# Moving one fetch in the opening, and the queues and buffers of the last regroupings and stores, in a fused Fourier-mixing and SoLU kernel

## The chip, the cores and the metric

The kernel runs on one core of a Trainium2 chip, in float32 throughout. The metric is the time of one execution on the device, in microseconds (us). The kernel before took 1618.07 us, the median of three runs (1616.99, 1618.07 and 1626.45).

## The reference

What is computed, cut to what matters: a circular convolution along the sequence by way of the real Fourier transform, and on its result a two-layer block with a SoLU activation and a layer norm.

```python
X = np.fft.rfft(x, axis=1)                  # x: 8 x 3136 x 256
y = np.fft.irfft(X * F, n=3136, axis=1)     # F = filt_r + 1j * filt_i
h = y.reshape(25088, 256) @ w_in            # d_ff = 1024
sm = exp(h - max(h)) / (sum(exp(h - max(h))) + 1e-9)
solu = h * sm
ln = (solu - mean(solu)) / sqrt(var(solu) + 1e-6) * g_ln
out = ln @ w_out                            # 25088 x 256
```

## The kernel before, in words

**Fourier part.** The sequence of 3136 is split as 49 x 64. Each batch element goes through four stages with two trips to DRAM: a first product with a 49-point table (`first`, matmul L230 or L273, results `d1` in DRAM), then for seven "units" of frequencies `forward` (product with a table `de`, matmul L305, tiles `pb`), `multiply` (by the filter, L326 to L328, tiles `pr`, `pi`, `pt`), `inverse` (L305 again, tiles `pc`, copied out by ScalarE at L343) and `store` (L347, `d2` in DRAM), and last `back` into the rows `y` that the second block reads.

**Opening.** For batch element 0 this runs on its own, ahead of everything else, in an order that is written out by hand (manual schedule). Its first unit's rows `t2` are asked for at L563 (16 DMAs, shared by SyncE's and ScalarE's queues). The other six units' rows are asked for on SyncE's queue at L295 (`y<-d`, 512 KB each, the last 128 KB), in the loop at L565. Between the second and the third pass of that loop, SyncE's queue also gets `load_tables(8, 5)`: one DMA for `de` (L471) and eight for the filters (L474), which units 4 to 6 need. TensorE's order is forward 0, 1, 2, inverse 0, forward 3, inverse 1, forward 4, inverse 2 and so on; VectorE does `multiply` i while TensorE does forward i+1 or i+2. In `inverse`, a matmul called `idle` (L538) writes the same PSUM tile first. `pr`, `pi` and `g` have two buffers each, so `multiply` i waits for `inverse` i-2. After the last unit VectorE unpacks the weights (L427 to L451), `back` fills `y`, and the main loop starts.

**Main loop.** 196 blocks of 128 tokens, in pairs (98 pairs, numbered 0 to 97). `step(k)` runs for k = 0 to 204; each step issues instructions for several blocks at different stages, and each engine does its own in that order. A pair p passes: product with `w_in` (L728, a seven-product scheme for two blocks at once), exponential, normalize (L776), square (L784), turn (a 32x32 transpose on VectorE, L792), `regroup` (L795, DMAs at L807: from `turn` to `solu_t`), `project_sums` on GpSimd (L707), `project` (L858, again seven products, of eight 128x128 matmul instructions each), `keep_out` on ScalarE (L871) and `finish_out` on VectorE (L875) into the tile `ot`, and `store_out` (L878, DMAs at L883).

`last` (L887) is the range of pairs 93 to 97.

**The end of the loop.** In step 198 the last two pairs are regrouped together: for pairs 96 and 97, two tiles each and four DMAs a tile, 128 KB a DMA, all on SyncE's queue, 16 in a row. Pair 97's tiles come from pool `r`, which has four buffers and is free by then. Pair p's seven products run in steps 2p+9 (products 1, 2, 6, 7) and 2p+10 (products 5, 3, 4). Products 1, 6 and 5 add into one PSUM tile, and ScalarE copies it out between them (`keep_out`), and then the part that belongs to the other output; so product 6 waits for the copy after product 1, and product 5 for the copy after product 6. Product 4 waits for VectorE's `finish_out`, which waits for ScalarE's copy after product 5. `ot` has two buffers in pool `wk2`: pair 96's writes wait until pair 94's `ot` has been stored. Pairs 93 to 96 are stored from GpSimd's queue, where the two DMAs stand between the sums of the next pairs, and all others from SyncE's.

**Landings.** Each DMA of SyncE's and ScalarE's queues tells its landing on one of eight semaphores (DMAHW0 to DMAHW7), which are dealt out in turn over both queues; an issue waits until the DMA before it on its own semaphore has landed. Such a wait holds the issuing engine's queue.

Of the kernel before, what the change touches and what calls it, by code (L numbers as in the profile page):

```python
# [9 lines left out]
FP32 = mybir.dt.float32  # L10
# [7 lines left out]
P = 128  # L18
B, S, C = 8, 3136, 256
# [10 lines left out]
NCH = 4  # L30
KD, KF = C // P, DFF // P
# [63 lines left out]
def kernel(  # L95
# [10 lines left out]
    nc = tc.nc  # L106
# [6 lines left out]
    rows = np.arange(P)[:, None]  # L113
    turn_dram = nc.inline_tensor(np.concatenate(
        [rows % 32 == np.arange(32), rows // 32 == np.arange(4)], 1).astype(np.float32),
        name="turn_tbl").ap()
# [289 lines left out]
    with ExitStack() as st:  # L406
# [157 lines left out]
                out=t2_0[NH * (n % 4):NH * (n % 4) + NH, n // 4, :], in_=rows_x[n:n + 1])  # L564
        for i in range(1, units):  # L565
            sp.fetch(i, nc.sync.dma_start, spare_piece(i - 1))
            if i == 2:
                load_tables(8, NP - 8, nc.sync.dma_start)
        for i in range(2):
            start(i)  # L570
# [52 lines left out]
    wk2 = pool("wk2", 2)  # L623
# [61 lines left out]
    def load_de(sp, u):  # L685
# [3 lines left out]
                            in_=de_dram[i:i + pairs].rearrange("i p k u q -> p i (k u q)"))  # L689
        return de  # L690

    turns, variances, solu_ts, solu_sums, spreads, rss, pos, ots, places = (
        {} for _ in range(9))
    sums, ms, hs, nmaxs, es, solus, squares = {}, {}, {}, {}, {}, {}, {}


# [95 lines left out]
        nc.vector.transpose(out=turns[g][:, :, i, :],  # L792
                            in_=solus[k].rearrange("p (f j) -> p f j", j=32))

    def regroup(p, i):  # L795


        g, second = divmod(p, 2)
        turned = turns[g].rearrange("p (k q) b i -> p k q (b i)", q=4)
        a = 2 * second + i  # L800
        if p == last[-1]:
            st = pools["r"].tile([P, KF, P], FP32, name=f"solu_t_{p}_{i}", tag="r")
        else:
            st = upool.tile([P, KF, P], FP32, name=f"solu_t_{p}_{i}", tag=f"solu_t{i}")
        solu_ts[p, i] = st[:, 0:KF // 2, :], st[:, KF // 2:KF, :]
        for q in range(4):
            nc.sync.dma_start(out=st[32 * q:32 * q + 32, :, :],  # L807
                              in_=turned[32 * a:32 * a + 32, :, q, :])

    def deviations(g):  # L810
        rs = small.tile([P, 4], FP32, name=f"rs_{g}", tag="rs", bufs=2)
# [31 lines left out]
    def project(p, m):  # L843

        alone = m == 3 and p in last
        bank = 2 if alone else {1: 0, 6: 0, 5: 0, 3: 0, 2: 1, 7: 1, 4: 1}[m]
        if alone:
            pos[p, bank] = ps_m.tile([P, DFF // 2], FP32, name=f"o{m}_{p}", tag="m0")[:, 0:P]
        elif m in (1, 2):
            ps = ps_o.tile([P, DFF // 2], FP32, name=f"o{m}_{p}", tag=f"o{bank}")  # L850
            pos[p, bank] = ps[:, 0:P]
            places[p] = ps[:, P:P + 4]
        s1, s2, s3, s4 = solu_sums[p]
        lhs = {1: solu_ts[p, 0][0], 2: solu_ts[p, 0][1], 4: solu_ts[p, 1][1], 5: s1, 6: s2, 7: s3,
               3: s4}[m]
        w = w_out_sb[:, {1: 0, 2: 1, 3: 2, 5: 3, 6: 4, 7: 5, 4: 6}[m]]
        for f in range(KF // 2):
            nc.tensor.matmul(out=pos[p, bank], lhsT=lhs[:, f, :], rhs=w[:, f, :],  # L858
                             start=f == 0 and (m in (1, 2, 7) or alone), stop=True,
                             skip_group_check=True)  # L860
# [2 lines left out]

    def out_half(p, i, n):
        if p not in ots:
            ots[p] = wk2.tile([P, 2, C], FP32, name=f"ot_{p}", tag="ot")
        return ots[p][:, i, P * n:P * n + P], rss[p // 2][:, 2 * (p % 2) + i:2 * (p % 2) + i + 1]

    def keep_out(p, i, to):
        rs = out_half(p, i, 0)[1]  # L870
        nc.scalar.activation(out=out_half(p, *to)[0], in_=pos[p, 0], func=AFT.Copy, scale=rs)  # L871
# [6 lines left out]
    def store_out(p):  # L878
        g, second = divmod(p, 2)

        rows = out[4 * P * g:4 * P * g + 4 * P, :].rearrange("(b a i) c -> a b i c", a=4, i=32)
        for i in range(2):
            (nc.gpsimd if p in last[:-1] else nc.sync).dma_start(out=rows[2 * second + i], in_=ots[p][:, i, :])  # L883
        del ots[p]

    blocks = NT * B // 2
# [77 lines left out]
    def step(k):  # L964
        j, odd = divmod(k, 2)
        p = j - (LAG - 1) // 2 if odd else j - (LAG + 1) // 2
        if not 0 <= p < pairs:
            p = None
        hid, proj = k < blocks, p is not None
        if not odd and 2 <= j - 4 < pairs:  # L970
            project_sums(j - 4, 0)
        if k < LAG:
            if not odd:
                product(j, 1)
                keep(j, k, 0)
                product(j, 2)
                finish(j, k, 0, (k, 0), 1)
            else:
                product(j, 5)
                keep(j, k - 1, 1)  # L980
                finish(j, k, 1, (k - 1, 1), 2)
        for job in top[k] + stores[k] + products[k]:
            job()
        if not odd and 0 <= j - 4 < 2:
            project_sums(j - 4, 0)
        if odd and j + 1 < pairs:
            pair_sums(j + 1)
        if not odd:
            if hid and k > LAG:
                product(j, 1)  # L990
                keep(j, k, 0)
            if 2 <= k < blocks:
                exponential(k - 2)
            if proj:
                project(p, 5)
                keep_out(p, 1, (1, 1) if p in last else (0, 1))
            if p in last:
                keep_out(p, 0, (0, 1))
                finish_out(p, 1, 1, (1, 1), 1)
            if blocks <= k < blocks + 2:  # L1000
                exponential(k - 2)
            if hid and k > LAG:
                product(j, 2)
            if 3 <= k < blocks + 3:
                turn(k - 3)
            if hid and k > LAG:
                finish(j, k, 0, (k, 0), 1)
            if proj and p not in last:
                finish_out(p, 1, 1, (0, 1), 1)
            for job in early[k]:  # L1010
                job()
            if 3 <= k < blocks + 3:
                square(k - 3)
            if hid:
                product(j, 6)
                keep(j, k + 1, 0)
            if proj:
                project(p, 3)
                if p not in last:
                    keep_out(p, 0, (0, 1))  # L1020
                project(p, 4)
            if j >= 4 and j % 2 == 0 and j - 4 < pairs:
                regroup_deviations((j - 4) // 2, places.pop(p) if proj else psum("ps_rs")[:, 0, 0:4])
            for job in spectrum_loads[k]:
                job()
            if 0 <= j - 3 < pairs - 1:
                for n in range(j - 3, pairs if j - 3 == pairs - 2 else j - 2):
                    regroup(n, 0)
                    regroup(n, 1)
            if 0 <= j - 4 < pairs:  # L1030
                project_sums(j - 4, 1)
            if 0 <= j - 3 < pairs and j % 2:
                deviations((j - 3) // 2)
            if hid:
                product(j, 7)
            if p in last:
                finish_out(p, 0, 1, (0, 1), 2)
                finish_out(p, 1, 0, (1, 0), 1)
                store_out(p)
            if 2 <= k < blocks + 2:  # L1040
                normalize(k - 2)
            for job in second_parts[k] + middle[k] + first_parts[k]:
                job()
            if proj and p not in last:
                finish_out(p, 1, 0, (1, 0), 1)
                store_out(p)
        else:
            if hid and k >= LAG:
                product(j, 5)
                keep(j, k - 1, 1)  # L1050
                finish(j, k, 1, (k - 1, 1), 2)
            for job in early[k]:
                job()
            if proj:
                project(p, 1)
                keep_out(p, 0, (0, 0))
                project(p, 2)
                finish_out(p, 0, 0, (0, 0), 1)
            if 2 <= k < blocks + 2:
                exponential(k - 2)  # L1060
            if hid:
                product(j, 3)
                product(j, 4)
            if proj:
                project(p, 6)
                project(p, 7)
            for job in second_parts[k] + middle[k]:
                job()
            if 3 <= k < blocks + 3:
                turn(k - 3)  # L1070
            if hid:
                finish(j, k - 1, 1, None, 0)
                finish(j, k, 0, (k, 0), 2)
            if 2 <= k < blocks + 2:
                normalize(k - 2)
            if proj:
                keep_out(p, 1, (1, 0))
            if 3 <= k < blocks + 3:
                square(k - 3)
            for job in first_parts[k]:  # L1080
                job()
        for job in late[k] + loads[k]:
            job()
        if k < 2:
            for n in ((0, 1), range(2, 7))[k]:
                prepare_w_out(n)
# [38 lines left out]
```

## Time and profile before

| | us |
|---|---|
| runs, median | 1618.07 |
| profiled execution | 1612.3 |
| its span | 1610.2 |
| TensorE busy in the span | 1552.6 (96%) |
| VectorE, GpSimd, ScalarE busy | 1316.2, 1196.3, 913.2 |
| TensorE idle from 53.08 on (opening) | 4.74 |
| TensorE idle from 1586.77 on (end) | 4.56 |
| last TensorE work ends, last output store is issued | 1605.1, 1605.5 |

The profiled execution is one execution on its own, 5.8 us shorter than the median of the three timed runs; times within it are compared with each other. In the profile, L12 is line 12 of the kernel; PE is TensorE, PEld its weight load, DVE VectorE, ACT ScalarE, POOL GpSimd and SP SyncE, and a "q" after the name is the engine's sequencer, which waits and issues DMAs. "[4.74 <-DMA y<-d]" says that the engine was idle for 4.74 us just before, and that the DMA from `d` to `y` ended it. PEclk is the share of its full clock that TensorE was granted.

### The profile page before, as it was taken

What the parts mean: (1) busy time and instruction counts of PE and PEld (TensorE: products, weight loads), DVE (VectorE), ACT (ScalarE), POOL (GpSimd) and SP (SyncE); (2) the same over time, 40 slices, a digit from 0 to 9 for tenths busy, and PEclk for the clock granted to TensorE, in tenths of its full rate; (3) what the DMA queues carried; (4) which work ended last, traced back from release to release, by engine and by line L of the source; (5) the groups of instructions that cost most, each with busy time, mean ns of one, the idle gap of its engine ahead of it and who ended that gap; (6) DMA issues with size and microseconds to landing.
All of it is one profiled execution on the core that took longest, in us unless ns stands there. A gap on an engine that the chain in (4) does not pass through costs nothing.

```text
span 1610.2 us, 37028 instructions
## 1 busy us (share of the span) xinstructions
PE 1552.6 (96%) x12808; PEld 1057.4 (66%) x12808; DVE 1316.2 (82%) x2635; ACT 913.2 (57%) x1821; POOL 1196.3 (74%) x1386
## 2 busy tenths in 40 slices
PE   5798899999999999999999999999999999999997
PEld 1362456666666676667766676667767777777776
DVE  1687887898899889987999789987898777777772
ACT  2135555566656656666565655666555665666662
POOL 4446998679777876886778877797776767677775
PEclk8999999999999999999999999999999999999999
DMA  9888878786887679866886678766774545344343
GB/s 274 245 267 246 251 219 237 210 228 199 216 258 235 180 200 257 236 181 164 229 240 206 169 194 254 202 189 176 219 222 125 141 118 133 86 113 110 106 112 99
DMA packets 342651, 311.94 MB, mean 194 GB/s; under 512 B 28922, under 2 KB 307987, under 8 KB 342467
## 3 DMA queue, kind: packets, MB, share of 16 engines
q1 hardware_dynamic: 268724, 167.37, 39.5%
q0 software_dynamic: 35648, 102.76, 21.1%
q10 hardware_dynamic: 38096, 39.46, 8.2%
q8 instruction: 104, 1.70, 0.5%
q14 instruction: 79, 0.65, 0.1%
HBM read 124.78 MB, written 81.40 MB: 128 GB/s over the span
## 4 chain that ended last, share of the span: by engine, by line
PE 66%; DMA 2%; DVE 1%; issue 1%; POOL 0%; SPq 0%; ACT 0%; DVEq 0%; POOLq 0%; ACTq 0%
PE o L858 30%; PE m L728 28%; PE py L376 3%; PE pc L305 2%; PE pa L273 2%; PE pb L305 2%; DMA solu_t<-turn 1%; DMA x<-in_x_dram 1%; DVE h L776 0%; DMA out_dram<-ot 0%; PE o L822 0%; DVE h L752 0%; SPq L807 0%; POOL u L707 0%; DVE h L749 0%
## 5 line engine op out<-in xcount | busy, mean ns | idle before, releaser
L858 PEld LDWEIGHTS o<-w_out_sb,solu_t 128*128 128x128 f32 x3136 | 382.4, 192 | 49.6 <-issue 43.5
L858 PE MATMUL o<-w_out_sb,solu_t 128*128 128x128 f32 x3136 | 402.2, 276 | 3.4 <-DVE ot L875 2.6
L728 PE MATMUL m<-w_in_sb,s 128*128 128x512 f32 x784 | 398.0, 608 | 3.4 <-ACT h L738 1.6
L858 PEld LDWEIGHTS o<-w_out_sb,u 128*128 128x128 f32 x2352 | 307.5, 192 | 141.8 <-issue 105.4
L776 DVE SCALAR_TENSOR_TENSOR h<-e,rsum,h 128x1024 f32<-128x1024 f32 x196 | 320.5, 1635 | 6.9
L858 PE MATMUL o<-w_out_sb,u 128*128 128x128 f32 x2352 | 311.8, 276 | 4.9 <-ACT ot L871 4.8
L728 PE MATMUL m<-w_in_sb,y 128*128 128x512 f32 x588 | 308.4, 608 | 5.0 <-DVE nmax L752 3.5
L738 ACT COPY h<-m 128x512 f32<-128x512 f32 x294 | 173.2, 589 | 203.3 <-PE m L728 194.2
L871 ACT ACTIVATE ot<-o,rs_t 128x128 f32<-128x128 f32 x392 | 143.2, 367 | 253.3 <-PE o L858 244.0
L707 POOL TENSOR_TENSOR u<-solu_t 128x512 f32<-128x512 f32 x98 | 137.8, 1406 | 165.5 <-DMA solu_t<-turn 114.5
L784 ACT ACTIVATE h<-h,nmu 128x1024 f32<-128x1024 f32 x196 | 224.8, 1147 | 48.6 <-DVE turn L792 38.1
L792 DVE STREAM_TRANSPOSE turn<-h 128x1024 f32<-128x1024 f32 x196 | 243.1, 1240 | 3.1
L752 DVE CUSTOM_DVE_ANT_0 h<-m,h 128x512 f32<-128x512 f32 x196 | 133.3, 680 | 128.1 <-ACT h L738 97.9
L760 ACT ACTIVATE e<-h,nmax 128x1024 f32<-128x1024 f32 x196 | 225.1, 1148 | 21.2 <-DVE h L776 19.8
L707 POOL TENSOR_TENSOR u<-solu_t,u 128x512 f32<-128x512 f32 x98 | 149.2, 1522 | 93.6 <-PE o L858 93.6
L728 PEld LDWEIGHTS m<-w_in_sb,s 128*128 128x128 f32 x784 | 127.8, 190 | 88.8 <-issue 67.1
L875 DVE SCALAR_TENSOR_TENSOR ot<-o,rs_t,ot 128x128 f32<-128x128 f32 x299 | 103.7, 347 | 78.4 <-ACT ot L871 59.9
L707 POOL TENSOR_TENSOR solu_t<-solu_t,solu_t 128x512 f32<-128x512 f32 x98 | 165.9, 1693 | 0.9
L728 PEld LDWEIGHTS m<-w_in_sb,y 128*128 128x128 f32 x588 | 96.6, 191 | 101.6 <-issue 55.6
L707 POOL TENSOR_TENSOR u<-u,solu_t 128x512 f32<-128x512 f32 x98 | 150.8, 1538 | 15.6 <-PE o L858 8.1
L707 POOL TENSOR_TENSOR s<-y 128x128 f32<-128x128 f32 x196 | 96.5, 493 | 0.5
L376 PEld LDWEIGHTS py<-wb_t,t 50*64 50x64 f32 x3584 | 57.6, 134 | 42.9 <-issue 19.4
(123 smaller groups left out, 2020.6 us busy)
## 6 DMA issues: line engine op xcount, KB each, us to landing
solu_t<-turn SPq DMA_DIRECT2D x784, 128.0 KB
out_dram<-ot SPq DMA_DIRECT2D x188, 128.0 KB
t<-d POOLq DMA_DIRECT2D x112, 200.0 KB, 6.9
d<-x POOLq DMA_DIRECT2D x100, 200.0 KB, 5.6
f<-f_dram POOLq DMA_DIRECT2D x39, 512.0 KB, 8.1
d<-g POOLq DMA_DIRECT2D x39, 512.0 KB, 5.0
t<-d ACTq DMA_DIRECT2D x37, 512.0 KB
x<-in_x_dram SPq DMA_DIRECT2D x112, 98.0 KB
```

Source lines behind the costliest of these rows:

```text
L376: nc.tensor.matmul(out=views[g][64 * h:64 * h + 64, cb, i, :], lhsT=t4[rows, i, c0:c0 + 64], rhs=wb_t[rows, 0:N1], start=True, stop=True)
L707: nc.gpsimd.tensor_tensor(out=out, in0=in0, in1=in1, op=op)
L728: nc.tensor.matmul(out=ms[j, bank], lhsT=lhsT, rhs=w_in_sb[:, w, :], start=m in (1, 2, 7), stop=True, skip_group_check=True)
L738: nc.scalar.copy(out=h_half(k, i), in_=ms[j, 0])
L752: nc.vector.tensor_tensor_reduce(out=h_half(k, i), in0=ms[j, bank], in1=h_half(*kept), scale=1.0, scalar=sofar, op0=ALU.add, op1=ALU.min, ...
L760: nc.scalar.activation(out=e, in_=hs[k], func=AFT.Exp, bias=nmaxs.pop(k)[:, 1:2], scale=-1.0, accum_out=esum)
L776: nc.vector.scalar_tensor_tensor(out=solu, in0=e, scalar=rsum, in1=solu, op0=ALU.mult, op1=ALU.mult, accum_out=nmu)
L784: nc.scalar.activation(out=solu, in_=solu, func=AFT.Square, bias=nmu, scale=-float(DFF), accum_out=variances[g][:, i:i + 1])
L792: nc.vector.transpose(out=turns[g][:, :, i, :], in_=solus[k].rearrange("p (f j) -> p f j", j=32))
L858: nc.tensor.matmul(out=pos[p, bank], lhsT=lhs[:, f, :], rhs=w[:, f, :], start=f == 0 and (m in (1, 2, 7) or alone), stop=True, skip_group_ ...
L871: nc.scalar.activation(out=out_half(p, *to)[0], in_=pos[p, 0], func=AFT.Copy, scale=rs)
L875: nc.vector.scalar_tensor_tensor(out=ot, in0=pos[p, bank], scalar=rs, in1=out_half(p, *kept)[0], op0=ALU.mult, op1=ALU.add)
```

## The change

In the opening, `load_tables` moves one pass later: the rows of unit 3 (the fourth of seven) are asked for ahead of the last tables and no longer behind them.

At the end, pair 97's second tile is no longer regrouped in step 198 from SyncE. Its four DMAs are issued from ScalarE's queue in step 199, two after the `keep_out` that follows product 1 of pair 95, two after the one that follows its products 6 and 7. Its first tile stays where it was.

The output tiles of pairs 96 and 97 are taken from pool `r` and not from `wk2`.

All output stores are issued from SyncE.

```diff
         for i in range(1, units):
             sp.fetch(i, nc.sync.dma_start, spare_piece(i - 1))
-            if i == 2:
+            if i == 3:
                 load_tables(8, NP - 8, nc.sync.dma_start)
...
-    def regroup(p, i):
+    def regroup(p, i, dma=nc.sync.dma_start, parts=range(4)):
...
-        for q in range(4):
-            nc.sync.dma_start(out=st[32 * q:32 * q + 32, :, :],
-                              in_=turned[32 * a:32 * a + 32, :, q, :])
+        for q in parts:
+            dma(out=regrouped[p, i][32 * q:32 * q + 32, :, :], in_=turned[32 * a:32 * a + 32, :, q, :])
...
         if p not in ots:
-            ots[p] = wk2.tile([P, 2, C], FP32, name=f"ot_{p}", tag="ot")
+            if p in last[-2:]:
+                ots[p] = pools["r"].tile([P, NCH, C], FP32, name=f"ot_{p}", tag="r")[:, 0:2]
+            else:
+                ots[p] = wk2.tile([P, 2, C], FP32, name=f"ot_{p}", tag="ot")
...
-            (nc.gpsimd if p in last[:-1] else nc.sync).dma_start(out=rows[2 * second + i], in_=ots[p][:, i, :])
+            nc.sync.dma_start(out=rows[2 * second + i], in_=ots[p][:, i, :])
...
                     regroup(n, 0)
-                    regroup(n, 1)
+                    if n != last[-1]:
+                        regroup(n, 1)
...
                 keep_out(p, 0, (0, 0))
+            if j == pairs + 1:
+                regroup(last[-1], 1, nc.scalar.dma_start, range(2))
+            if proj:
                 project(p, 2)
...
                 keep_out(p, 1, (1, 0))
+            if j == pairs + 1:
+                regroup(last[-1], 1, nc.scalar.dma_start, range(2, 4))
```

More of the change, by code (lines that the diff above doesn't have):

```diff
@@ L690, in load_de @@
         return de
-    turns, variances, solu_ts, solu_sums, spreads, rss, pos, ots, places = (
-        {} for _ in range(9))
+    turns, variances, solu_ts, solu_sums, spreads, rss, pos, ots, places, regrouped = (
+        {} for _ in range(10))
     sums, ms, hs, nmaxs, es, solus, squares = {}, {}, {}, {}, {}, {}, {}
@@ L800, in regroup @@
         a = 2 * second + i
[L801 to L805, printed above, removed]
-        for q in range(4):
-            nc.sync.dma_start(out=st[32 * q:32 * q + 32, :, :],
-                              in_=turned[32 * a:32 * a + 32, :, q, :])
+        if (p, i) not in regrouped:
+            if p == last[-1]:
+                st = pools["r"].tile([P, KF, P], FP32, name=f"solu_t_{p}_{i}", tag="r")
+            else:
+                st = upool.tile([P, KF, P], FP32, name=f"solu_t_{p}_{i}", tag=f"solu_t{i}")
+            regrouped[p, i] = st
+            solu_ts[p, i] = st[:, 0:KF // 2, :], st[:, KF // 2:KF, :]
+        for q in parts:
+            dma(out=regrouped[p, i][32 * q:32 * q + 32, :, :], in_=turned[32 * a:32 * a + 32, :, q, :])
     def deviations(g):
@@ L865, in out_half @@
         if p not in ots:
-            ots[p] = wk2.tile([P, 2, C], FP32, name=f"ot_{p}", tag="ot")
+            if p in last[-2:]:
+                ots[p] = pools["r"].tile([P, NCH, C], FP32, name=f"ot_{p}", tag="r")[:, 0:2]
+            else:
+                ots[p] = wk2.tile([P, 2, C], FP32, name=f"ot_{p}", tag="ot")
         return ots[p][:, i, P * n:P * n + P], rss[p // 2][:, 2 * (p % 2) + i:2 * (p % 2) + i + 1]
```

## The prediction

> **What bounds the kernel now.** The page first: TensorE is busy for 96% of the span. Of 1610.2 us that leaves 58 us in which it waits, so a change that takes no matmul away can only shorten a wait or the work ahead of the matmuls. The chain of waits that ended last is next; its last pieces, in order of time:
>
> ```profile
> 1583.85 0.51 POOL out_dram L883
> ...
> 1584.59 6.04 DMA out_dram<-ot
> ...
> 1590.82 0.38 ACT ot L871
> ...
> 1591.33 13.77 PE o L858 x96
> ```
>
> A store is issued on GpSimd, takes 6.04 us to land, ScalarE writes the freed `ot`, and 96 matmuls follow without a break. The timeline of those microseconds says what it costs:
>
> ```profile
> 1590.82 0.37 ACT L871 ACTIVATE ot<-o,rs_t 128x128 f32<-128x128 f32 x1 [5.74 <-DMA out_dram<-ot]
> 1591.33 2.05 PE L858 MATMUL o<-w_out_sb,u 128*128 128x128 f32 x8 [4.56 <-ACT ot L871]
> 1593.17 1.92 PE L858 MATMUL o<-w_out_sb,solu_t 128*128 128x128 f32 x8
> ...
> 1600.24 1.06 PE L858 MATMUL o<-w_out_sb,u 128*128 128x128 f32 x8
> ```
>
> TensorE stands 4.56 us; then eight matmuls take 2.05 and 1.92 us where later eight take 1.06. The table by stretches shows why: of the last three figures, the granted clock comes first, then the DMA engines' share and GB/s:
>
> ```profile
> 1591.30:1597.40 6.10, 6.07 (x32) 6.01 (x32) 0.61 (x2) 0.99 (x3) 3.93 (x4) 0.59 0.30 74
> 58.00:66.00 8.00, 8.00 (x60) 3.55 (x63) 2.17 (x4) 1.07 (x2) 0.98 (x1) 0.64 0.66 221
> ```
>
> The second row is the opening, where TensorE had also stood. There the timelines of TensorE, SyncE and VectorE read:
>
> ```profile
> 57.81 2.01 PE L305 MATMUL pb<-y,de 64*64 64x256 f32 x16 [4.74 <-DMA y<-d]
> 42.60 0.36 SPq L471 DMA_DIRECT2D de<-de_tbl  x1
> 52.89 11.08 SPq L295 DMA_DIRECT2D y<-d  x4
> 63.79 0.69 DVE L326 TENSOR_TENSOR pr<-pb,f 128x512 f32<-128x512 f32 x1 [6.23 <-PE pc L305]
> ```
>
> The rows of unit 3 are asked for at 52.89, after the tables begun at 42.60. They end TensorE's wait at 57.81, and `inverse` 1 behind it ends VectorE's at 63.79. From there VectorE is the bound of the opening: busy 13.72 of 14 us in 66 to 80 and 24.38 of 25 in 80 to 105, until its first work of the main loop (L752, 111.19). What it gains at 63.79 therefore comes out at the start of the main loop, and every engine behind it moves along.
>
> **What the Trainium skill says.** "TensorE: Matmul & The Clock Gate", Part 1: after an idle window of about 3.4 us (the windows run free) TensorE gets half its clock until a busy one has passed. The trace agrees: clock records show 0.5 from 1589.47 to 1596.30 and from 56.89 to 63.71, two windows each; a stop of 1.84 us at 136.67 also brought one window of 3.41. "DMA: Bandwidth & Descriptors", Issuing engines are not separate DMA queues: DMAs of all queues share 16 engines, another queue saves only time to issue. The trace agrees: regroups behind each other on SP land 2.3 to 2.5 us after issue; four issued at 1583.86 to 1586.15 beside GpSimd's stores took 5.4 to 6.5. The same page, Anatomy of one DMA: a semaphore wait happens on the issuing sequencer. Here one of SP's fetches waited 9.2 us for a store of ScalarE's queue.
>
> **The change part by part.** The program order of both kernels, with waits, is compared; TensorE's and VectorE's orders are the same. The sum is made against the profiled 1612.3.
>
> *Opening, fetch of unit 3.* It takes the tables' place on SP: issue 42.60 and not 52.89. Unit 2's rows landed at 47.91, 1.44 after unit 1's, so unit 3's should at 49.4. Forward 3 can then follow `inverse` 0 at 53.1 (before 57.8). `inverse` 1 is next; it needs GpSimd's `pi`, done at 55.8, so ends near 56.7 (before 63.7). Forward 4 needs unit 4's rows: the same bytes are ahead of them in the queue as before, so they land about when they did, 59.0, or some tenths later: 59.3 (TensorE got to it at 63.5). Forward 5 was at 66.59. Its rows were asked for at 53.92, and are now not: by the new rotation SP's issue for unit 5 waits on the semaphore of ScalarE's first `g` store, as only unit 6's did (63.64). That store goes out at 54.20 as before, and landed at 63.62; now it has one fetch of 512 KB less ahead of it, and nothing of unit 5. Bounds: 59 and 63.6. I take 60. A loaded fetch took 4.8 to 5.7 us, a lone one 2.0: unit 5's rows at 63.5 to 66, against 66.59, a gain of 0.6 to 3.1. With 63.7 the gain is 3.0. But TensorE's stop before forward 4 (56.7 to 59.3) is 2.6 us; if it brings a half-clock window, forward 4 and `inverse` 2 take about twice their 3 us, unit 5's rows are no longer what is late, and 1.8 are left. I take the middle, 2.4, ends 0 and 4.2 (VectorE's `multiply` 4 cannot end earlier than 65.9, where `multiply` 5 began at 70.10). Nothing was lost by the tables' delay of 1.4 us: `multiply` 4 needs them at 62.7, and their last piece should land near 57.
>
> *Last `ot` in pool `r`.* The 5.74 us wait on ScalarE goes. What is late next at this place is GpSimd's `u2` of pair 96, done at 1587.93 before, so alone this is worth 1591.33 - 1587.9 = 3.4 us, and the half clock: 96 matmuls at 0.89 us per eight (starts 1600.24, 1601.13 and 1602.03 in the timeline) are 10.7, with the last drain 10.9, where 13.77 were used: 2.9 us.
>
> *Stores on SP.* GpSimd loses eight issues of 0.69 to 0.81 us. Pair 93's stores go behind pair 95's regroup on SP (1572.4), where the queue then waits for VectorE's turn until 1577.67 anyway: free. Pair 94's stand behind pair 97's first tile, near 1585.7, no longer in the midst of the regroups. SP's other stores find it empty, and the last one is issued after VectorE's last instruction as before. Gain: pair 95's sums start some 2.5 us earlier, of which TensorE waited 0.15 and 0.26 only; pair 96's are held by their own regroup (landing 1584.8), so nothing: I count 0.
>
> *Four regroups on ScalarE.* They save SP four issues at its end (1586.15 to 1590.63), but ScalarE pays. Each waits for its semaphore: the second and fourth quarter of pair 96's first tile (landed 1580.81 and 1582.14 before) and of its second tile (1583.48 and 1584.82). Queued behind are the `keep_out`s that ran at 1580.68 and at 1582.80. With 0.6 us for an issue (SP's regroups 0.62, ScalarE's own issues so far 0.31 to 0.60) the first pair ends at 1582.75: `keep_out` at 1583.1, TensorE's product 5 at 1583.2 and not 1581.6, a stop of 2.0 us. The 16 engines now serve two queues (the DMA share was 0.7 to 0.8 with one), so I put 0.5 us on the later landings: last issue ends at 1585.9, two copies to 1586.35, VectorE's `finish_out` to 1586.7: product 4 at 1586.7 and not 1583.60. From there the old pace: product 6 of pair 96 at 1586.77 + 3.1 = 1589.9, 1.4 us before 1591.33. All sums are there by then (1587.5 to 1590.2). With warm TensorE 10.9 us more: 1600.8 against 1605.1, a gain of 4.3. The two stops of 2.0 and 1.7 us may bring a half-clock window, worth 1.7: three in ten, 0.5 off. Tail: 3.8, ends 6.3 (no wait on ScalarE, 3.4 + 2.9) and -1.
>
> Pair 97's second tile lands by 1588.5, when GpSimd is still at pair 96's sums; before, it was waited for until 1593.8.
>
> Sum: 2.4 + 3.8 = 6.2. Profiled 1612.3 - 6.2 = 1606.1; the runs 1618.07 - 6.2 = 1611.9.
>
> **The rivals.** *A. As summed*, both parts: 1611.9.
> *B. The opening gives nothing back.* Unit 5's rows come with the first store's landing at 63.6 plus 3: 66.6, as before. For it: that store landed 9.4 us after its issue. Against: 512 KB less are queued ahead. 1618.07 - 3.8 = 1614.3.
> *C. No wait on ScalarE*, or hidden: 3.0 + 6.3: 1608.8. For it: TensorE has slack until 1587.9. Against: the program order names the four waits, and pair 96's landings are in the trace.
> *D. The end does nothing*: the wait moves whole from the store to ScalarE's issues, and TensorE goes cold again: only the opening, 1615.7.
> *E. Slower.* The same place as D, but longer: the fourth quarter of pair 96's second tile, on which ScalarE's last issue waits, lands so late under two queues that everything behind it is later than before. Its landing plus 4.6 is product 6 of pair 96 (1585.3 and 1589.9 above); plus 10.9, plus 2.5 for a cold clock, is TensorE's end. That is 1605.1 + 2.4, so that the opening is eaten too, at a landing of 1589.5: 7.1 us after its issue at 1582.44. The longest regroup near there took 6.5, lone ones 2.4. At 8 us: 1619.0.
>
> **How the numbers follow.** A 0.55, B 0.17, C 0.14, D 0.08, E 0.06. The forecast is A's, 1611.9. From C less the scatter of the two lower runs (1 to 2 us) to a D with a slow run: 1606.5 to 1618.5. One per cent is 16 us, about what can be told from no change here. No case comes near it, and only runs like the 1626.45 among three could: faster 0.02, same 0.95, slower 0.03.
>
> **What would show it.** Right: forward 3 starts by 53.5, and the wait on `y<-d` moves to forward 4 or 5; VectorE's first `pr` after its wait starts before 60; L752's first instruction near 109. At the end no wait of ScalarE on `out_dram<-ot`, two waits of TensorE of 1 to 2.5 us within pair 95, eight matmuls of pair 96 in 1.06 us, a clock of 1.00 in the last 20 us. Wrong: unit 5's fetch issued after 63; a stop of TensorE above 3.4 us at the end; PEclk near 0.6 there; a landing of pair 96's regroup over 5 us.

## The result, and the profile after

The changed kernel took 1612.48 us (median of 20 runs), the kernel before 1615.94 (20 runs, the three known ones among them). The ratio is 0.9981, with a 95% interval of 0.9968 to 0.9994: 3.1 us gained, between 1.0 and 5.2. (The ratio is worked out over all runs and is not the quotient of the medians.) The forecast was 1611.9, but from 1618.07: a gain of 6.2. The profiled execution took 1613.62 us (span 1611.6), *longer* than the profiled one of before (1612.3). So from here on the whole time is read from the timed ratios, and the profile only stretch by stretch, each measured from a mark inside it.

The lines of the changed kernel are numbered a little higher (L807 is L809, L858 L859, L871 L875, L875 L879, L883 L887). The last pieces of the chain of waits, to hold against those of before:

```profile
1575.11 3.58 DMA solu_t<-turn
...
1580.56 1.29 POOL u L707
1586.01 2.99 DMA solu_t<-turn
1590.47 1.16 PE o L859 x8
1591.74 14.68 PE o L859 x112
```

The store of `ot` and its 6.04 us are gone from it. In their place stands the landing of a regroup, 2.99 us, on which ScalarE's last issue waited. The timeline of the same place, ScalarE and TensorE:

```profile
1584.32 1.93 ACTq L809 DMA_DIRECT2D solu_t<-turn  x2
1586.30 0.37 ACT L875 ACTIVATE ot<-o,rs_t 128x128 f32<-128x128 f32 x1 [3.72 <-DMA solu_t<-turn]
1586.72 2.05 PE L859 MATMUL o<-w_out_sb,u 128*128 128x128 f32 x16 [1.97 <-ACT ot L875]
1587.59 2.02 ACTq L809 DMA_DIRECT2D solu_t<-turn  x2
1589.66 0.63 ACT L875 ACTIVATE ot<-o,rs_t 128x128 f32<-128x128 f32 x2 [2.99 <-DMA solu_t<-turn]
1590.47 1.16 PE L859 MATMUL o<-w_out_sb,solu_t 128*128 128x128 f32 x8 [1.70 <-DVE ot L879]
1591.60 3.50 PE L859 MATMUL o<-w_out_sb,solu_t 128*128 128x128 f32 x16
1595.99 1.06 PE L859 MATMUL o<-w_out_sb,solu_t 128*128 128x128 f32 x8
```

The two pairs of issues hold ScalarE for 3.72 and 2.99 us, and TensorE stops for 1.97 and 1.70 us behind them, both within pair 95, as forecast. The 16 matmuls at 1591.60 (pair 96, products 1 and 2) take 3.50 us where 16 took 2.03 in the kernel before: a half-clock window, 1591.90 to 1595.31. In the table by stretches it is the 0.61 of the first row (granted clock, then DMA share, then GB/s); the second row is the opening:

```profile
1591.60:1596.00 4.40, 4.40 (x28) 4.40 (x27) 0.70 (x2) 0.53 (x2) 3.89 (x4) 0.61 0.31 72
58.00:66.00 8.00, 4.61 (x37) 1.92 (x39) 3.46 (x6) 0.81 (x2) 3.02 (x3) 0.80 1.00 337
```

The opening in the timelines of SyncE, VectorE, TensorE and VectorE again:

```profile
54.74 8.14 SPq L295 DMA_DIRECT2D y<-d  x3
58.25 0.67 DVE L326 TENSOR_TENSOR pr<-pb,f 128x512 f32<-128x512 f32 x1
61.39 1.12 PE L305 MATMUL pb<-y,de 64*64 64x256 f32 x16 [3.68 <-DVE pi L326]
66.23 0.69 DVE L326 TENSOR_TENSOR pr<-pb,f 128x512 f32<-128x512 f32 x1 [4.74 <-PE pc L305]
```

Forward 3 now starts at 52.88, without a stop, and VectorE's `multiply` 3, which ended a stop of 6.23 us at 63.79 before, runs at 58.25. But TensorE stops one unit later, before forward 4, for 3.68 us (2.6 were forecast). The name in the brackets is misleading: that `pi` ended at 60.89; the rows of unit 4 landed at 61.30, 0.09 us ahead of forward 4, and 0.09 us lie between these two in runs 1, 3 and 5 as well. VectorE then stops for 4.74 us.

The two stretches in this one pair of profiles. Times at the end are counted from the start of VectorE's last turn (L792, 1576.44 before and 1579.82 after); "forward 0" is the first `pb` of the opening (44.69 and 46.51).

| us | before | after | forecast |
|---|---|---|---|
| turn to product 5 of pair 95 | 5.26 | 6.90 | +1.6 |
| turn to product 4 of pair 95 | 7.16 | 10.65 | +3.1 |
| turn to product 6 of pair 96 | 14.89 | 15.08 | -1.4 |
| from there to TensorE's end | 13.76 | 11.51 | -2.9 |
| turn to VectorE's last work ("the end") | 29.04 | 26.98 | -3.8 |
| forward 0 to first L752 ("the opening") | 66.50 | 64.31 | -2.4 |
| first L752 to last turn (the main loop) | 1465.25 | 1468.99 | 0 |

The end and the opening both look right here, and the main loop, in which nothing differs but the queue of pair 93's two stores, is 3.7 us longer. That is why the experiments were needed.

### The profile page after: what moved, and what is told of

It reads as the page before. It is cut to its first block, busy times and chain, and to the rows that moved or that the text cites. A ratio compares the mean times of both kernels' runs of the same rounds, so it can differ in the third digit from the quotient of the medians.

```text
span 1611.6 us, 37022 instructions
## 1 busy us (share of the span) xinstructions
PE 1554.8 (96%) x12808; PEld 1058.1 (66%) x12808; DVE 1321.1 (82%) x2635; ACT 912.1 (57%) x1821; POOL 1189.6 (74%) x1378
## 5 line engine op out<-in xcount | busy, mean ns | idle before, releaser
L859 PEld LDWEIGHTS o<-w_out_sb,solu_t 128*128 128x128 f32 x3136 | 383.5, 193 | 53.2 <-issue 43.5
L859 PE MATMUL o<-w_out_sb,solu_t 128*128 128x128 f32 x3136 | 403.7, 277 | 6.0 <-DVE ot L879 5.2
L859 PEld LDWEIGHTS o<-w_out_sb,u 128*128 128x128 f32 x2352 | 306.2, 192 | 139.4 <-issue 105.9
L776 DVE SCALAR_TENSOR_TENSOR h<-e,rsum,h 128x1024 f32<-128x1024 f32 x196 | 324.3, 1655 | 6.9
L859 PE MATMUL o<-w_out_sb,u 128*128 128x128 f32 x2352 | 310.4, 275 | 2.4 <-ACT ot L875 2.3
L875 ACT ACTIVATE ot<-o,rs_t 128x128 f32<-128x128 f32 x392 | 143.0, 366 | 250.1 <-PE o L859 239.8
L792 DVE STREAM_TRANSPOSE turn<-h 128x1024 f32<-128x1024 f32 x196 | 243.1, 1240 | 3.1
L752 DVE CUSTOM_DVE_ANT_0 h<-m,h 128x512 f32<-128x512 f32 x196 | 133.2, 680 | 126.6 <-ACT h L738 96.4
L707 POOL TENSOR_TENSOR solu_t<-solu_t,solu_t 128x512 f32<-128x512 f32 x98 | 169.4, 1729 | 0.9
L879 DVE SCALAR_TENSOR_TENSOR ot<-o,rs_t,ot 128x128 f32<-128x128 f32 x299 | 103.6, 347 | 76.5 <-ACT ot L875 52.6
L707 POOL TENSOR_TENSOR u<-u,solu_t 128x512 f32<-128x512 f32 x98 | 147.7, 1508 | 15.6 <-PE o L859 8.6
```

Of the source, the lines that this page charges most:

```text
L707: nc.gpsimd.tensor_tensor(out=out, in0=in0, in1=in1, op=op)
L752: nc.vector.tensor_tensor_reduce(out=h_half(k, i), in0=ms[j, bank], in1=h_half(*kept), scale=1.0, scalar=sofar, op0=ALU.add, op1=ALU.min, ...
L776: nc.vector.scalar_tensor_tensor(out=solu, in0=e, scalar=rsum, in1=solu, op0=ALU.mult, op1=ALU.mult, accum_out=nmu)
L792: nc.vector.transpose(out=turns[g][:, :, i, :], in_=solus[k].rearrange("p (f j) -> p f j", j=32))
L879: nc.vector.scalar_tensor_tensor(out=ot, in0=pos[p, bank], scalar=rs, in1=out_half(p, *kept)[0], op0=ALU.mult, op1=ALU.add)
```

## The experiments

**The theory.** The end gains 2 to 4 us: the buffer takes away the long stop, and ScalarE's regroups give a part back. **The rival** for the opening: its gain is only the luck of one pair of profiles, and the bytes on the way to forward 5 are what bounds it. Each ratio below is to the kernel before on the same chip (its medians were 1614.72, 1617.2, 1617.72 and 1616.26 us for runs 1 to 4, 5 to 8, 9 to 11 and 12), with its 95% interval; runs 7 and 8 have a profile alone. Each stretch comes from one profile.

**1. The opening alone.** The kernel before, with `if i == 3` and nothing else.

> The kernel before with the opening's edit alone. In the trace, from TensorE's first forward matmul to VectorE's first row maximum of the main loop (L752), before had 66.5 us and the changed kernel 64.3. Theory (the gain of the opening is real, and limited by unit 5's rows, whose issue waits for the first g store's landing): 64.3 within 0.7 here too, and the last part, from VectorE's last turn to its last instruction, stays at 29.0 as before. Rival (the difference of 2.2 us was scatter of the DMAs): near 66.5. Time: 2 to 3.5 us less than before, if what the opening gains is kept.

Measured: 1.0005 of before (0.9984 to 1.0026). Its profile has the opening at 70.11 us, longer than any other, because TensorE stood before forward 4 until 65.36 and then ran at half clock:

```profile
65.36 2.01 PE L305 MATMUL pb<-y,de 64*64 64x256 f32 x16 [6.28 <-issue]
```

Unit 4's rows had landed at 65.27, 8.46 us after their issue. The end is that of before, 30.06. No gain is to be seen, but the interval alone would still hold the 2.4 us that were forecast (0.9985); the table of openings below speaks against them.

**2. The end alone.** The changed kernel with `if i == 2`.

> The changed kernel without the opening's edit: only the regroups on ScalarE, the free output buffers and the stores on SyncE. From VectorE's last turn to its last instruction before had 29.0 us, the changed kernel 27.0. Theory: 27.0 within 1 here (25.7 if no half-clock window falls on the end, 27.5 if a longer one does); the opening as before, 66.5. Time: 2 to 3 us less than before.

Measured: 0.9986 (0.9972 to 0.9999), within the uncertainty that of the whole change. The end takes 25.35: product 6 of pair 96 comes 13.64 us after the turn (forecast for the change: 13.5), and 11.31 to TensorE's end. Here the half-clock window began at 1585.36: products 5 and 3 of pair 95 took 3.66 us and filled what was the second stop, so that it cost next to nothing. The gain only just clears the noise; the medians of this run and of before, 1614.18 and 1614.72, stand closer than the ratio says. The opening, the old one, takes 64.39, as short as in the changed profile.

**3. All regroups on SyncE.**

```diff
-                    if n != last[-1]:
-                        regroup(n, 1)
+                    regroup(n, 1)
...
-            if j == pairs + 1:
-                regroup(last[-1], 1, nc.scalar.dma_start, range(2))
...
-            if j == pairs + 1:
-                regroup(last[-1], 1, nc.scalar.dma_start, range(2, 4))
```

> The changed kernel with the last tile's four regroups back on SyncE behind the other twelve, so that nothing stands in ScalarE's queue; the free output buffers, the stores on SyncE and the opening stay. Theory (ScalarE's waits for landings before its four issues cost 3.5 us of the path and bring the half clock): from VectorE's last turn to its last instruction 22.7 us, where the changed kernel has 27.0: product 6 of pair 96 starts 11.0 us after the turn and not 15.1, with no half-clock window. Rival (the landings of pair 97's last tile or GpSimd's sums hold the end anyway, and ScalarE's issues were the price of having them early): 26 to 27. Time by the theory: 8 us less than before, 4 less than the changed kernel; by the rival the changed kernel's.

Measured: 0.9984 (0.997 to 0.9998); the end takes 24.19. Timelines of TensorE and GpSimd in that run:

```profile
1594.73 1.16 PE L859 MATMUL o<-w_out_sb,u 128*128 128x128 f32 x8 [1.48 <-POOL u L707]
1599.27 1.27 POOL L707 TENSOR_TENSOR u<-solu_t 128x512 f32<-128x512 f32 x1 [2.14 <-DMA solu_t<-turn]
```

Both stops of 2 us are gone, product 5 is at 4.77 and product 6 of pair 96 at 11.32. That is 3.8 us earlier than with ScalarE's share (15.08), so the four regroups there cost more than they save. The remainder missed the forecast (12.48 to TensorE's end, where about 11.3 was expected): GpSimd waited 2.14 us for pair 97's second tile, whose last quarter is now the last of 16 on one queue. Run 5, without this wait, has 11.74.

**4. The kernel before, again,** as a control.

> The kernel before once more, as a control of how far one profile of the same program lies from another. From the first row maximum to the last turn the profile of before has 1465.3 us and that of the changed kernel 1469.0, though the two programs are the same there. If that is scatter, this one lies 1 to 4 us from 1465.3 as well; the opening 66.5 and the end 29.0 within 0.7, if these two are steady.

Measured: 1.0002 (0.999 to 1.0015). Its profile: opening 64.62, end 28.20. Against the 66.50 of the first profile, the *same* opening is 1.9 us shorter, nearly the whole 2.4 that the change was forecast to gain there. The main loop, 1465.87, lies within 0.7 us of the first, less than the 1 to 4 expected; how far it scatters shows over all the profiles, below.

**5. Pair 97's second tile first.** As 3, with the order on SyncE turned round.

```diff
-                    regroup(n, 0)
-                    regroup(n, 1)
+                    for i in ((1, 0) if n == last[-1] else (0, 1)):
+                        regroup(n, i)
```

> The changed kernel with all regroupings on SyncE's queue, pair 97's second tile now ahead of its first (GpSimd's sum of pair 97's last product needs the second tile alone; the first is needed some 4 us later). If the end is set by the copies on ScalarE and by that one tile, product 6 of pair 96 starts 11.3 us after VectorE's last turn and TensorE ends 10.9 to 11.4 later: 22.5 to 23.0 us from the turn to VectorE's last work, where the order first-second gave 24.19. Rival: the landings of these eight DMAs are late as a whole, whatever their order; then product 1 of pair 97 waits for the first tile and the stretch stays at 24 or more. Opening as in the change: 64.3 to 70.1 from the first forward product to the first row maximum.

Measured: 0.9953 (0.9935 to 0.9972); the end takes 23.42, 0.4 above the forecast and 0.8 below run 3. GpSimd's first sum of pair 97 no longer has a wait ahead of it:

```profile
1596.00 1.16 PE L859 MATMUL o<-w_out_sb,u 128*128 128x128 f32 x8 [1.45 <-POOL u L707]
1598.36 1.27 POOL L707 TENSOR_TENSOR u<-solu_t 128x512 f32<-128x512 f32 x1
```

So the rival (all of the landings late) falls. The timed step from run 3 is larger than 0.8 us in 1616 explains; the two intervals touch, the two runs were on different chips, each with its own before, and the rest is not explained.

**6. The opening's first store behind the last fetches.** As 5, and

```diff
-            sp.store(i, nc.scalar.dma_start)
+            sp.store(i, nc.scalar.dma_start if i else nc.sync.dma_start)
```

> As the last one, and the first store of the opening (g_0, 512 KB) is issued from SyncE, behind the fetches of units 5 and 6, where the change has it on ScalarE beside unit 4's fetch. Theory: unit 4's rows land 6.6 to 8.5 us after their issue in the changed opening because this store shares the transfer with them, and unit 5's fetch then waits for the store's landing. If so, unit 4's rows land 4.8 to 5.5 us after their issue, unit 5's fetch is issued within 1 us of it, TensorE's stop before forward 4 falls under 2.5 us, and the first forward product to the first row maximum takes 61.5 to 63 us. Rival: the bytes of the tables ahead of unit 4's rows set their landing; then it stays at 6.5 or more and the stretch at 64.3 or more.

Measured: 0.9954 (0.9939 to 0.997), no different from run 5. In its profile the first half is as expected: unit 4's rows land 5.05 us after issue, unit 5's fetch follows in 0.8 us, TensorE's stop is 1.66, forward 5 comes 15.6 us after forward 0 (19.5 in the changed profile). The second half is not: the opening takes 65.04. TensorE's and ScalarE's timelines:

```profile
59.63 1.12 PE L305 MATMUL pb<-y,de 64*64 64x256 f32 x16 [1.66 <-DMA y<-d]
66.36 1.07 ACT L343 COPY g<-pc 128x512 f32<-128x512 f32 x2 [7.30 <-DMA d<-g]
67.00 2.08 PE L538 MATMUL pc<-f,de 128*128 128x512 f32 x2 [3.24 <-ACT g L343]
```

ScalarE's copy of unit 2 waits for a store of `g` (g_0's landed at 65.93, g_1's at 66.28), TensorE waits for the copy, 3.24 us, and loses its clock. The stop was moved once more.

**7. The buffer alone.** The kernel before with pool `r` for the last two `ot`; stores and regroups as before.

> The kernel before with one edit: the output tiles of pairs 96 and 97 from pool r. Theory: this buffer alone is the gain at the end. Product 6 of pair 96 still 14.9 us after VectorE's last turn, then 10.9 to 11.4 us to TensorE's end where before took 13.0 to 13.8, so 26.0 us from the turn to VectorE's last work (before: 28.2 to 30.1). Rival: the regroupings on ScalarE bring the gain; then it stays at 28 or more.

**8. ScalarE's regroups alone.** The change without its other three edits.

> The kernel before with one edit: pair 97's second tile regrouped from ScalarE's queue in two halves as in the change (old buffers, old queues of the stores). Theory: the four regroupings move the stops from one place to another: product 5 of pair 95 at +6.9, product 4 at +10.65, product 6 of pair 96 at 13.6 to 15.1 after the last turn where before has it at 14.9, and the last part 13.0 to 13.8 as before; 27.0 to 29.5 in all, no gain above 1 us over before's 28.2 to 30.1. Rival: they carry the gain; then the stretch is 26.5 or less.

Measured: 27.25 and 29.49 for the end, where 26.0 and 27.0 to 29.5 were expected. In run 7 product 6 of pair 96 already comes at 11.57 and not at 14.9, as nothing delays ScalarE any more. But then the rest takes 15.29:

```profile
1599.11 1.26 POOL L707 TENSOR_TENSOR u<-solu_t 128x512 f32<-128x512 f32 x1 [3.63 <-DMA solu_t<-turn]
1601.76 1.16 PE L858 MATMUL o<-w_out_sb,u 128*128 128x128 f32 x8 [2.95 <-POOL u L707]
```

GpSimd's stores of pair 94, issued at 1587.61 and 1588.35, stand beside the last regroups: those before them land 2.3 to 2.4 us after issue, the seven behind 4.1 to 6.7. Pair 97's sums wait 3.63 us for their tile, and TensorE 2.95. The kernel before had this as well (GpSimd waited 2.09 us for pair 97's tile), unseen, since TensorE was late by its own stop. In run 3, with the stores on SyncE, only pair 97's last quarter was as late as 4.13. In run 8 both waits stand behind each other, ScalarE's on its semaphores and then the old one on the store, and the half clock follows:

```profile
1585.78 0.62 ACT L872 ACTIVATE ot<-o,rs_t 128x128 f32<-128x128 f32 x2 [3.01 <-DMA solu_t<-turn]
1591.76 0.37 ACT L872 ACTIVATE ot<-o,rs_t 128x128 f32<-128x128 f32 x1 [3.70 <-DMA out_dram<-ot]
1592.27 2.05 PE L859 MATMUL o<-w_out_sb,u 128*128 128x128 f32 x8 [2.52 <-ACT ot L872]
```

**9. The store between fetch 4 and fetch 5.** As 6; units 5 and 6 are asked for after g_0's store.

```diff
-        for i in range(1, units):
+        for i in range(1, units - 2):
...
             sp.store(i, nc.scalar.dma_start if i else nc.sync.dma_start)
+            if i == 0:
+                for n in range(units - 2, units):
+                    sp.fetch(n, nc.sync.dma_start, spare_piece(n - 1))
```

> As the run with g_0's store on SyncE behind the last fetches, but the store stands between unit 4's fetch and unit 5's there. That run showed unit 4's rows landing in 5.05 us and forward 5 at 15.6 us after forward 0, and then a new wait of TensorE before forward 6 (g's buffer, held until g_0's store landed at 65.9). Theory: the order fetch 4, store, fetch 5 serves all three: unit 4's rows within 5.5 us of issue, g_0 stored by 62, unit 5's rows by 63.5; forward 6 three us after forward 5, and 59.5 to 61.5 us from the first forward product to the first row maximum (64.3 to 70.1 in the changed opening, 62 to 67 in the old). Rival: transfers are full up to there, and what one gains another loses; then the stretch is 64 or more. Whole time: 0.993 to 0.996 of before.

**10. The first raw weights one unit later.** As 9, with `begin(2)` at i = 2.

> As the last one, and GpSimd's first load of raw weights (512 KB, issued at 56.5 us while the rows are under way) comes one unit later. If its bytes slow unit 5's rows and the stores, forward 5 and the first row maximum come up to 1 us earlier than in the last one; rival: it goes after them anyway, and nothing moves by more than 0.3 us, or the conversion of these weights, now later, delays the first product by up to 1 us.

**11. That opening with the old end.** The kernel before with the opening of 9.

> The kernel before with the opening of the run that has the store between the fetches, and no other edit (the end as before). The opening's moved fetch alone gave 1.0005 of before. If an opening that ends its stretch at 60 to 61.5 us after the first forward product is passed on to the end, the whole is 3 to 5 us shorter than before: 0.997 to 0.998. Rival: the main loop takes it back (its spread over profiles is 9 us); then 0.999 or more.

Measured: 0.9931 (0.9905 to 0.9956), 0.9949 (0.9929 to 0.997) and 0.9979 (0.9963 to 0.9994). The openings take 64.14, 66.23 and 64.99 us, none of them the 60 to 61.5 expected. In run 9:

```profile
65.53 1.12 PE L305 MATMUL pb<-y,de 64*64 64x256 f32 x16 [1.68 <-DMA y<-d]
66.54 1.07 ACT L343 COPY g<-pc 128x512 f32<-128x512 f32 x2 [6.83 <-DMA d<-g]
```

g_0's store lands in time (62.03), but unit 5's rows only at 65.40, 8.67 us after their issue: what the store gains the rows lose, as the rival said. ScalarE's copy of unit 2 starts 0.08 us after g_1's store has landed (66.46), with g_0's landed long before. Run 10's later load does not help: unit 5's rows take 8.79. Run 11's ratio is better than run 1's, by 0.0026; that suggests a gain of some 4 us for this opening over the change's, but the intervals overlap and the chips differ. The ratios of runs 9 and 11 lie where they were expected, but not by way of the opening: run 11's interval leaves out 1 although its opening, 64.99, is no shorter than the old ones (63.7 to 66.8). Where that gain sits, the profiles do not show.

**12. A third buffer for `g`,** with the rest as in 6.

> The run with g_0's store on SyncE behind the last fetches, and one buffer more (three) for g in the opening. There, and in the run with the store between the fetches, ScalarE's copy of unit 2 stood until 0.1 us after a store of g had landed (66.3 and 66.5), and TensorE and VectorE behind it. If that is g's buffer, the wait goes: forward 6 three us after forward 5, and 60 to 61.5 us from the first forward product to the first row maximum; the whole 0.992 to 0.994 of before. Rival: it is the stores' semaphore and no buffer; then the copy still starts at a store's landing, and the stretch stays at 64 to 66.

Measured: 0.9953 (0.9939 to 0.9967). The opening takes 67.11. A shorter one was not seen, as unit 4's rows landed 8.09 us after issue in this execution, the last 4.4 of them with g_1's store under way from ScalarE's queue:

```profile
65.47 2.01 PE L305 MATMUL pb<-y,de 64*64 64x256 f32 x16 [5.62 <-DMA y<-d]
71.41 1.07 ACT L343 COPY g<-pc 128x512 f32<-128x512 f32 x2 [10.46 <-PE pc L305]
```

ScalarE waited for TensorE, and all stores had landed. What the waits of 6 and 9 were for can be read from the semaphores in the traces: there the copy of unit 2 has a wait of its own line (L343) on the semaphore of g_1's store, which ended at 66.30 and 66.48, and the copy of unit 3 one on that of g_0's store. With a third buffer the copy of unit 2 waits for no store. So it was the buffer, and the one that g_1's store holds. What its removal gains stays open.

**The openings side by side,** every profile there is, in us. The issue of unit 4's rows and the forwards are counted from forward 0, "flight" is from that issue to the rows' landing:

| order of the opening | unit 4 issued | flight | forward 3 | forward 4 | forward 5 | opening |
|---|---|---|---|---|---|---|
| old: before, 4, 2, 7, 8, mean | 7.7 | 6.1 | 12.3 | 17.4 | 20.4 | 65.2 |
| range | 6.3-8.7 | 5.5-7.3 | 11.4-13.1 | 16.0-18.8 | 19.0-21.9 | 63.7-66.8 |
| changed: after, 1, 3, 5, mean | 9.7 | 7.3 | 7.5 | 17.2 | 22.5 | 67.4 |
| range | 8.2-11.1 | 6.6-8.5 | 6.4-8.5 | 14.9-19.6 | 19.5-25.3 | 64.3-70.1 |
| store on SyncE: 6, 9, 10, 11, 12, mean | 8.4 | 6.3 | 7.1 | 14.9 | 19.7 | 65.5 |
| range | 7.4-9.8 | 5.1-8.1 | 6.1-9.2 | 12.6-16.6 | 15.6-22.3 | 64.1-67.1 |

## Why the prediction was right, and where it was not

**The total.** 1611.9 stands beside 1612.48, but the forecast's gain was 6.2 us and the measured one is 3.1 (1.0 to 5.2). The three runs that it started from have a median 2.1 us above that of the 20, and this covers much of the missing gain: that the number came so close is luck. In its outcome the result is rival B: the end pays, and of the opening no gain was seen.

**The end, mechanism right, two terms mis-sized.** "From there the old pace: product 6 of pair 96 at 1586.77 + 3.1" was 13.5 us after the turn; run 2 shows 13.64, the changed profile 15.08. The difference is the half-clock window, given "three in ten, 0.5 off": it came in both profiles with two stops of 2 us, and cost about 1.5 us where it fell on products 1 and 2. The remainder, put at 10.9 us for a warm TensorE, took 11.31 in run 2, at full clock throughout. The landings on which ScalarE's last issues waited took 2.96 and 2.99 us, as forecast (2.4 and 0.5 more). The whole end: 28.2 to 30.1 in four profiles with before's end (before, 1, 4, 11; mean 29.1), 27.0 and 25.4 with the change's: 2.9 us on the mean, 3.8 forecast. The timed ratio of run 2, 0.9986, is 2.3 us (0.2 to 4.5).

**The end, wrongly credited.** "Stores on SP: I count 0" is wrong. It holds only while TensorE waits for `ot`; once the buffer is free, the stores issued from GpSimd cost 3 us (27.25 in run 7, 24.19 in run 3); whether by their queue, or by standing among the regroups in time, was not separated. The prediction saw that pair 97's second tile came earlier, and put it to ScalarE's regroups. These gain nothing alone (run 8: 29.49), and with the other edits they cost 1.2 to 2.8 us (24.19 without, 25.4 and 27.0 with them). The buffer alone is worth 1.9 (29.1 to 27.25), not the 3.4 + 2.9 that were put on it.

**The opening, the step that failed** is "the same bytes are ahead of them in the queue as before, so they land about when they did". Forward 3 did move, by 4.8 us on the mean. But SyncE's queue issues unit 4's fetch 2.0 us later on the mean and its flight is 1.2 us longer, so forward 4 comes when it did (17.2 and 17.4), and forward 5, whose rows are asked for only when g_0's store has landed (within 0.03 us in the changed profile and in runs 1, 3 and 5), 2.1 us later. For the flight of these rows the prediction went down to "a lone one 2.0"; but that was unit 6's fetch, of 128 KB. Unit 5's 512 KB took 4.0 to 4.6 us in those four profiles, with only unit 6's behind them on the queue. (Its "With 63.7 the gain is 3.0" should be 2.9, from 66.59.) The step fits the one changed profile, in which forward 4 comes at 14.9, the earliest of four. It was also set against the one profile of before that has the second longest old opening. Of the Trainium skill, "DMA: Bandwidth & Descriptors", Issuing engines are not separate DMA queues, is what the runs bear out: between 58 and 66 us the 16 engines are busy for 1.00 of the time, at 337 GB/s, and putting one transfer ahead puts another back. That a full transfer is *the* cause of the longer flights is argued from this row; what makes one execution's flight 5 us and another's 8 was not found.

The half-clock window that the prediction allowed for came in each of them: 3.4 or 6.8 us of it about forward 4, in the changed profile and in runs 1, 3 and 5. The claim that what VectorE gains is passed on holds as far as the first L752: from forward 5 to it all profiles but one have 44.5 to 45.3 us (49.4 in run 6, with its stop in between). Beyond it nothing can be told from single profiles: the main loop scatters from 1461.2 to 1471.3 us over all 14.

**Its signs.** Right: forward 3 by 53.5; `pr` before 60; two stops of 1 to 2.5 us in pair 95; no wait on `out_dram`; unit 5's fetch before 63 (61.81); no stop over 3.4 us at the end. Wrong: L752 near 109 (110.82; counted from forward 0 it is 64.31, 2.2 less than before, but the three other profiles with this opening have 67.3 to 70.1), and a clock near 0.6 at the end did come.

**A faster version.** All regroups on SyncE, pair 97's second tile first, stores on SyncE and the buffer: 0.9953, 0.9954, 0.9931, 0.9949 and 0.9953 of before in five versions (runs 5, 6, 9, 10, 12) that differ in their openings: 7 to 11 us shorter. Of this the end explains 5.7 us (29.1 to 23.4); where the rest comes from is not shown. The end takes 23.4 in four of them, 24.95 in run 12, where a half-clock window fell into it. The intervals of runs 9 and 12 end below that of the change (0.9968 to 0.9994), the others overlap with it by 0.0004 at most. Which of the openings is best was not settled.

## What to carry to other kernels

Before a wait is costed from one profile, ask how much the same stretch differs in a second profile of the same kernel: here it was 1.9 us for an opening in which 2.4 were to be gained, and, with the DMA engines full, moving one transfer ahead only moved the stop to the next. An edit that costs nothing beside a long stop is to be costed again with that stop removed, together with the edit that removes it. A DMA handed to a compute engine's queue can bring that queue the wait for an older transfer's semaphore: here 3.72 and 2.99 us for two issues each, and the stops of TensorE behind them cost a clock window too.

## What the runs showed that was not expected

- TensorE lost its clock without standing for a whole window. In the changed profile the window that began at 1591.90 followed 3.41 us in which it stood for 1.70 only, and 1.65 in the 3.41 before. The Trainium skill ("TensorE: Matmul & The Clock Gate", Part 1) speaks of an idle window of about 3.4 us; here half of one was enough. In each of the 14 traces all half-clock windows begin on one grid of 3.41 us. Of the full-clock stretches of that grid between 40 and 1600 us, all 39 with 1.80 us or more of standing were followed by half clock, 8 of the 38 with 1.45 to 1.80, and none of those with less. So at the same place a stop of 1.48 us brought a half-clock window in run 12 and none in run 3. The first stop in pair 95 brought one in run 2, where its 1.96 us fell into one stretch of the grid, and none in the changed profile, where 1.65 of its 1.97 did.
- Regroups of 128 KB that take 2.3 to 2.4 us alone on SyncE's queue took 4.1 to 6.7 with two stores of the same size issued from GpSimd among them (run 7), and 2.3 to 2.4 for 15 of 16 when the stores stood behind them on SyncE (run 6, the last one 4.16).
- The same 512 KB fetch, unit 4's, took 5.5 to 7.3 us over the five profiles with the old order of the opening, and 6.6 to 8.5 over the four with the changed one.
